# Pooled attention and a gated conv FFN: a ninth conv quarter moves from TensorE to VectorE, under a new order of all engines

## Chip, cores and metric

One Trainium2 chip, one core. The metric is the device time of one execution in microseconds (us); lower is better. Engines are named as in the profile: PE is TensorE's matmuls, PEld its weight loads, DVE is VectorE, ACT is ScalarE, POOL is GpSimd, SP is SyncE.

## What is computed

Eight sequences, each with 8 heads, 576 positions and 64 columns per head. Attention in which keys and values are averaged over groups of 8 positions (so 72 of each per head), and behind it a feed-forward part whose hidden layer is gated by a 3-tap convolution of itself along the sequence:

```python
k_p = k.reshape(B, H, 72, 8, D).mean(axis=3)
v_p = v.reshape(B, H, 72, 8, D).mean(axis=3)
scores = scale * q @ k_p.transpose(0, 1, 3, 2)
attn = softmax(scores)                      # over 72 pooled keys
x = heads_side_by_side(attn @ v_p)          # 8 x 576 x 512
h = relu(x @ w_in)                          # 512 -> 1024
conv = sum(conv_w[t] * shift(h, t - 1) for t in range(3))   # per channel, along the sequence
out = (h * sigmoid(conv)) @ w_out           # 1024 -> 512
```

Inputs and output are f32 in HBM (q, k, v are 9.4 MB each, the output too); the work inside is in bf16 with f32 sums.

## The kernel before, in words

Everything goes by sequence b (0 to 7), and two sequences make a group g that shares a tile gT for the gated hidden layer; channels lie on partitions in blocks fb of 128, positions along the free axis. Four blocks are a **quarter** (b, f4): f4 = 0 holds blocks 0 to 3, f4 = 1 blocks 4 to 7. So 16 quarters of conv in all, two for each sequence.

Attention for a sequence: q, k and v come by loads on POOL's queue (L285, L292, L318, L321; some raw f32 by SP at L300, cast at L307). DVE averages pairs of positions (keys L465; values L512, then L516 masks them). TensorE transposes q (L542, or L546 in smaller pieces) and L560 copies the result from PSUM on DVE or ACT. Scores are matmuls of L608 (16 small ones) or L621 (4 large ones). DVE takes row maxima (L634) and subtracts (L646); ACT takes exponentials (L683). The weights are transposed on TensorE (L693, copied at L707) or by DMA. L718 multiplies by the pooled values, L731 takes the reciprocals of the sums, L746 (DVE) or eight L739 (ACT) divide. L763 transposes x and L771 copies it, again on DVE or ACT; later groups do it by DMA.

FFN for a sequence: `ffn_in` (L776, 64 matmuls 128x288: eight blocks, two half sequences, four pieces of the 512 inputs), `ffn_relu` on ACT (L785) into hT. The convolution of a quarter then has two forms:

- **On TensorE**: `ffn_conv`, two calls per quarter, each 32 matmuls of 64x64 diagonals (L940) over hT. ACT squashes from PSUM (four L965); half the channels land on the other partitions and go to a tile tg first. DVE adds 1 (one L980 for the straight half, two L982 for the crossed one).
- **Taps on DVE**: the ends of each half sequence are first copied beside it (`ffn_wrap`, L860 and L861, two wraps per quarter, on POOL or ACT), then for each block two scalar_tensor_tensor (`ffn_tap`, L912, eight per quarter) sum h·ratio + h into f32 in tg. ACT squashes from tg with the weight as scale (`ffn_tap_tanh`, four L922), and `ffn_tap_gate` (one L927) adds 1.

The tables `Graph.TAPS` (quarters whose taps are on DVE), `Graph.WRAP` (sequences whose hT holds the wrapped ends) and `Graph.SIG` (all quarters of sequences 5 to 7: squashed by a sigmoid itself, so that no 1 is added) say which. Both forms end in `ffn_times` (L990, DVE, gate times h for a quarter). The last matmul L998 takes a group's 128-row tiles, eight matmuls each; L1009 copies the sum from PSUM on DVE or ACT (into osb, or into spare qp buffers), and L1021 stores it. L425 are fillers: matmuls on nothing that keep TensorE going.

Nothing decides at run time. All operations form a graph with dependences, and `Graph.order` emits them in a fixed list, `ORDER`: each number is 2 × operation + choice of engine (where an operation can run on two), −1 a filler. `FORMS` picks forms of scores and transposes, `PLACES` the buffer that each tile gets. An engine's instructions run strictly in the order of that list, so it sets who stands behind whom on each queue. Buffers per ring: tg 3, hT 2, gT 2, v 3, kk 1, qp 4, osb 5.

Of the kernel before, what the change touches and what calls it, by code (L numbers as in the profile page):

```python
# [33 lines left out]
class Graph:  # L34
# [24 lines left out]
    WRAP = (4, 5, 6, 7)  # L59
    TAPS = ((4, 0), (4, 1), (5, 0), (5, 1), (6, 0), (6, 1), (7, 0), (7, 1))  # L60
# [123 lines left out]
def kernel(  # L184
# [1125 lines left out]
    def add_ffn(b, w):  # L1310
# [38 lines left out]
        for f4 in range(n_fb // 4):  # L1349
            if (b, f4) not in Graph.TAPS:  # L1350
                continue
# [148 lines left out]
```

## Time and profile before

| | |
|---|---|
| median of 3 runs | 211.93 us (211.72 to 212.32) |
| the profiled execution, its own time | 211.99 us |
| its span in the trace | 210.3 us |
| granted TensorE clock, mean | 0.996 |
| busy PE / PEld / DVE / ACT / POOL | 199.0 / 135.0 / 191.6 / 170.5 / 43.0 us |
| HBM read / written | 32.52 / 9.44 MB |

The span is what the trace covers, 1.7 us less than the time. Busy time counts instructions of an engine, without the ones that only wait or issue. A matmul is pipelined, so what it counts as busy may include a wait for its place; a step (the time of a run of equal matmuls by their number) is the better measure. In a row "idle before" is the engine's time without work just ahead of the instruction, with what ended it.

### The profile page before, as it was taken

What the parts mean: (1) busy time and instruction counts of PE and PEld (TensorE: products, weight loads), DVE (VectorE), ACT (ScalarE), POOL (GpSimd) and SP (SyncE); (2) the same over time, 40 slices, a digit from 0 to 9 for tenths busy, and PEclk for the clock granted to TensorE, in tenths of its full rate; (3) what the DMA queues carried; (4) which work ended last, traced back from release to release, by engine and by line L of the source; (5) the groups of instructions that cost most, each with busy time, mean ns of one, the idle gap of its engine ahead of it and who ended that gap; (6) DMA issues with size and microseconds to landing.
All of it is one profiled execution on the core that took longest, in us unless ns stands there. A gap on an engine that the chain in (4) does not pass through costs nothing.

```text
span 210.3 us, 6742 instructions
## 1 busy us (share of the span) xinstructions
PE 199.0 (95%) x2764; PEld 135.0 (64%) x2764; DVE 191.6 (91%) x341; ACT 170.5 (81%) x352; POOL 43.0 (20%) x72
## 2 busy tenths in 40 slices
PE   4999999979999999999999999999999999999990
PEld 1567788756688876766768864675577556644450
DVE  7899897999999989999999989999999999999741
ACT  3558886996999889999878999999999998878110
POOL 8823061042311120000000133040026005120000
PEclk9999999999999999999999999999999999999998
DMA  6999999999999999964955865667368547106985
GB/s 205 229 205 208 206 207 208 207 208 205 208 228 206 207 207 202 139 143 84 161 97 104 94 152 115 90 139 149 43 141 183 116 97 180 42 0 141 222 230 158
DMA packets 48835, 33.48 MB, mean 159 GB/s; under 512 B 28300, under 2 KB 43812, under 8 KB 48804
## 3 DMA queue, kind: packets, MB, share of 16 engines
q0 software_dynamic: 15216, 15.40, 44.2%
q1 hardware_dynamic: 32272, 15.67, 36.8%
q10 hardware_dynamic: 1316, 1.98, 3.6%
q8 instruction: 21, 0.34, 0.6%
q14 instruction: 10, 0.08, 0.1%
HBM read 32.52 MB, written 9.44 MB: 200 GB/s over the span
## 4 chain that ended last, share of the span: by engine, by line
PE 63%; DVE 11%; ACT 10%; DMA 8%; issue 4%; ACTq 1%; SPq 0%; DVEq 0%
PE psum L776 21%; PE psum L998 20%; PE psum L718 5%; PE psum L940 5%; DVE negm L634 4%; DVE sd L646 3%; DMA hT<-in_k_dram 3%; DMA out_dram<-qp 3%; PE psum L425 2%; DMA eT<-e 2%; PE psum L608 2%; ACT hT L785 2%; PE psum L693 2%; ACT x L739 2%; PE psum L763 1%
## 5 line engine op out<-in xcount | busy, mean ns | idle before, releaser
L776 PE MATMUL psum<-xT,w_in_sb 128*128 128x288 bf16 x512 | 70.5, 286 | 0.1
L998 PE MATMUL psum<-w_out_sb,gT 128*128 128x512 bf16 (+1 forms) x296 | 67.4, 373 | 0.2 <-DVE gT L990 0.2
L776 PEld LDWEIGHTS <-w_in_sb 128*128 128x128 bf16 x512 | 48.0, 98 | 14.7 <-issue 0.8
L785 ACT ACTIVATE hT<-psum 128x576 bf16<-128x576 f32 x64 | 41.7, 664 | 6.1 <-PE psum L776 5.8
L998 PEld LDWEIGHTS <-gT 128*128 128x128 bf16 x296 | 27.8, 98 | 27.9 <-DVE gT L990 0.7
L860 POOL COPY hT<-hT 128x126 bf16<-128x126 bf16 x13 | 10.2, 786 | 94.2 <-ACT hT L785 90.0
L634 DVE TENSOR_REDUCE negm<-psum 128x8 f32<-128x576 f32 (+2 forms) x37 | 27.4, 746 | 2.1 <-PE psum L608 1.2
L922 ACT ACTIVATE gT<-tg,ratio 128x576 bf16<-128x576 f32 x32 | 25.2, 803 | 2.5 <-DVE tg L912 2.3
L912 DVE SCALAR_TENSOR_TENSOR tg<-hT,ratio 128x576 f32<-128x576 bf16 x32 | 25.5, 813 | 0.7 <-ACT gT L922 0.4
L912 DVE SCALAR_TENSOR_TENSOR tg<-hT,ratio,tg 128x576 f32<-128x576 bf16 x32 | 25.0, 810 | 0.0
L739 ACT ACTIVATE x<-psum,r 128x64 bf16<-128x64 f32 (+1 forms) x96 | 21.2, 357 | 0.4 <-DVE r L731 0.4
L990 DVE TENSOR_TENSOR gT<-gT,hT 128x2304 bf16<-128x2304 bf16 x16 | 21.3, 1346 | 0.1
L646 DVE TENSOR_TENSOR sd<-psum,negm 128x576 f32<-128x576 f32 x27 | 19.9, 747 | 0.6
L718 PE MATMUL psum<-vm,eT 128*128 128x65 bf16 (+5 forms) x240 | 18.7, 222 | 0.4 <-DMA eT<-e 0.4
L683 ACT ACTIVATE e<-sd 128x576 bf16<-128x576 f32 x27 | 18.8, 717 | 0.0
L718 PEld LDWEIGHTS <-eT 128*128 128x128 bf16 (+1 forms) x240 | 15.1, 101 | 4.0 <-DMA eT<-e 0.7
L746 DVE TENSOR_TENSOR x<-psum,r 128x512 bf16<-128x512 f32 (+1 forms) x25 | 16.8, 683 | 0.3
L1009 ACT COPY osb<-psum 128x512 f32<-128x512 f32 x26 | 15.6, 632 | 0.9 <-PE psum L998 0.8
L940 PE MATMUL psum<-hT,dw 64*64 64x288 bf16 (+2 forms) x512 | 15.4, 255 | 0.6 <-ACT hT L785 0.3
L425 PE MATMUL psum<-gT 128*128 128x448 bf16 x40 | 12.8, 419 | 2.8 <-DVE gT L1107 2.8
L940 PEld LDWEIGHTS <-dw 64*64 64x64 bf16 x512 | 12.8, 107 | 2.5 <-issue 2.0
L512 DVE TENSOR_TENSOR v<-v 128x1280 bf16<-128x1280 bf16 (+2 forms) x24 | 12.8, 535 | 0.3
(95 smaller groups left out, 236.5 us busy)
## 6 DMA issues: line engine op xcount, KB each, us to landing
out_dram<-osb SPq DMA_DIRECT2D x54, 128.0 KB, 2.4
v<-in_v_dram POOLq DMA_DIRECT2D x8, 512.0 KB, 16.8
qp<-in_q_dram POOLq DMA_DIRECT2D x7, 576.0 KB, 17.3
kk<-in_k_dram POOLq DMA_DIRECT2D x3, 1152.0 KB, 15.2
out_dram<-qp ACTq DMA_DIRECT2D x14, 128.0 KB, 2.7
hT<-in_k_dram SPq DMA_DIRECT2D x2, 576.0 KB, 5.2
w_in_sb<-in_moe_w_in_dram POOLq DMA_DIRECT2D x2, 512.0 KB, 17.3
w_out_sb<-in_moe_w_out_dram POOLq DMA_DIRECT2D x1, 1024.0 KB, 18.0
```

Of the source, the lines that this page charges most:

```text
L634: nc.vector.tensor_reduce(out=a["m"][0:rows], in_=a["s"][0:rows, :, 0:2 * KW].rearrange("p a (h s) -> p a h s", s=Sp), axis=AX.X, op=OP.ma ...
L646: nc.vector.tensor_tensor(out=a["d"][0:rows], in0=a["s"][0:rows, :, 0:2 * KW].rearrange("p a (h s) -> p a h s", s=Sp), in1=a["m"][0:rows]. ...
L683: nc.scalar.activation(out=dst, in_=src, func=ACT.Exp,)
L718: nc.tensor.matmul(out=a["o"][lo:hi, h // 4, (h % 4) * (D + 1):(h % 4 + x1 - x0) * (D + 1)], lhsT=a["eT"][:, j, lo:hi], rhs=buf("vm", b)[: ...
L739: nc.scalar.activation(out=a["x"][0:rows, n * D:(n + 1) * D], in_=ov[:, n // 4, n % 4, 0:D], func=ACT.Identity, scale=r[0:rows, n // 4, n ...
L776: nc.tensor.matmul(out=banks(ps)[:, j, 0:SC], lhsT=w_in_block(dc, fb), rhs=buf("xT", g)[:, dc, i * S + j * SC:i * S + (j + 1) * SC], start ...
L785: nc.scalar.activation(out=h_of(b)[:, fb].rearrange("p (a s) -> p a s", a=2), in_=banks(ps)[:, :, 0:SC], func=ACT.Relu, scale=1.0 if (b, f ...
L912: nc.vector.scalar_tensor_tensor(out=acc, in0=h, scalar=w, in1=acc if tap else mid, op0=OP.mult, op1=OP.add)
L922: nc.scalar.activation(out=gate, in_=acc_of(b, fb, ps), func=squash(b, fb), scale=ratio[:, 1, fb:fb + 1])
L940: nc.tensor.matmul(out=banks(pss[r ^ c])[c * D:(c + 1) * D, j, lo:hi], lhsT=dw[r * D:(r + 1) * D, tap * n_fb + fb, :], rhs=hT[r * D:(r + 1 ...
L990: nc.vector.tensor_tensor(out=gate, in0=gate, in1=h_of(b)[:, four], op=OP.mult)
L998: nc.tensor.matmul(out=bank(ps)[0:rows, columns], lhsT=buf("gT", g)[:, fb, t * P:t * P + rows], rhs=w_out_sb[:, fb, columns], start=(fb == 0),
```

## The change

It puts quarter (3, 1), the second of sequence 3, into `TAPS`, and sequence 3 into `WRAP`. `ORDER`, `FORMS` and `PLACES` are other tables throughout, found anew; the code that reads them is the same. The diff without the three tables:

```diff
-    WRAP = (4, 5, 6, 7)
-    TAPS = ((4, 0), (4, 1), (5, 0), (5, 1), (6, 0), (6, 1), (7, 0), (7, 1))
+    WRAP = (3, 4, 5, 6, 7)
+    TAPS = ((4, 0), (4, 1), (5, 0), (5, 1), (6, 0), (6, 1), (7, 0), (7, 1), (3, 1))
...
     ORDER = (
-        0, 16, 4, 24, 44, 12, 14, 10, 36, -1, -1, -1, -1, -1, -1, 42, 8, 38, 34, 32,
```

What the two lists hold on each engine, where it differs:

| line | before | after |
|---|---|---|
| L940 PE (conv) | 512 | 448 |
| L542 / L546 PE (q transposed) | 72 / 288 | 126 / 180 |
| L608 / L621 PE (scores) | 376 / 56 | 408 / 44 |
| L425 PE (fillers) | 40 | 40 |
| L912 DVE (taps) | 64 | 72 |
| L927 / L980 / L982 DVE (+1) | 2 / 8 / 16 | 3 / 7 / 14 |
| L922 / L965 ACT (squash) | 32 / 32 | 36 / 28 |
| L860 and L861, POOL | 13 each | 14 each |
| L860 and L861, ACT | 3 each | 4 each |
| L771 DVE / ACT, 512 columns | 5 / 12 | 1 / 16 |
| L560 DVE / ACT, 1152 columns | 4 / 6 | 2 / 8 |
| L560 DVE, 512 columns | 2 | 1 |
| L307 DVE | a q cast, 512 columns | a k cast, 1152 columns |
| L707 DVE, 320 columns | 0 | 1 |
| L1009 DVE / ACT, 512 columns | 7 / 28 | 4 / 31 |

Three places show what moved. The first is DVE where sequence 3's stage begins. The tiles hT_116 and hT_117 are the two buffers of hT, gT_121 and gT_122 of gT; negm and sd are a row maximum and the shifted scores, kk and v the pooled pairs of keys and values. Before, from the second multiply of the sequence ahead of it on:

```order
L990 TENSOR_TENSOR gT_121<-gT_121,hT_116 128x4x576
L634 TENSOR_REDUCE negm_97<-psum 128x8
L465 TENSOR_TENSOR kk_78<-kk_78 128x9x256
L646 TENSOR_TENSOR sd_130<-psum,negm_97 128x576
L465 TENSOR_TENSOR kk_78<-kk_78 128x9x128
L512 TENSOR_TENSOR v_87<-v_87 128x5x128
L634 TENSOR_REDUCE negm_95<-psum 128x8
```

After, from the same multiply on (hT's two buffers have changed places):

```order
L990 TENSOR_TENSOR gT_121<-gT_121,hT_117 128x4x576
L634 TENSOR_REDUCE negm_96<-psum 128x8
L912 SCALAR_TENSOR_TENSOR tg_120<-hT_116,ratio 128x576
L912 SCALAR_TENSOR_TENSOR tg_119<-hT_116,ratio 128x576
L646 TENSOR_TENSOR sd_128<-psum,negm_96 128x576
L912 SCALAR_TENSOR_TENSOR tg_120<-hT_116,ratio,tg_120 128x576
L912 SCALAR_TENSOR_TENSOR tg_119<-hT_116,ratio,tg_119 128x576
L731 RECIPROCAL r_113<-psum 128x8
```

Four of the eight new taps stand between a row maximum and the work of the next tiles; the pooling of kk comes later. The second place is DVE where sequence 3's quarters are gated and multiplied. Before:

```order
L990 TENSOR_TENSOR gT_122<-gT_122,hT_117 128x4x576
L731 RECIPROCAL r_113<-psum 128x8
L512 TENSOR_TENSOR v_88<-v_88 128x5x64
L746 TENSOR_TENSOR x_110<-psum,r_113 128x512
L980 TENSOR_SCALAR gT_122<-gT_122 128x2x576
L982 TENSOR_SCALAR gT_122<-tg_119 64x2x576 x2
L990 TENSOR_TENSOR gT_122<-gT_122,hT_117 128x4x576
```

After:

```order
L980 TENSOR_SCALAR gT_122<-gT_122 128x2x576
L982 TENSOR_SCALAR gT_122<-tg_118 64x2x576 x2
L731 RECIPROCAL r_113<-psum 128x8
L912 SCALAR_TENSOR_TENSOR tg_119<-hT_116,ratio,tg_119 128x576
L990 TENSOR_TENSOR gT_122<-gT_122,hT_116 128x4x576
L516 TENSOR_TENSOR vm_90<-v_88,mask_wide 128x15x64
L927 TENSOR_SCALAR gT_122<-gT_122 128x4x576
L990 TENSOR_TENSOR gT_122<-gT_122,hT_116 128x4x576
```

The second quarter's +1 is now one L927 and its last tap stands ahead of the first quarter's multiply. The third place is the loads on POOL's queue in the head, after the first keys of sequence 1. Before:

```order
L285 DMA qp_74<-in_q_dram 128x4x576
L285 DMA qp_76<-in_q_dram 128x4x576
L328 DMA w_in_sb_67<-in_moe_w_in_dram 128x4x512
L318 DMA v_88<-in_v_dram 128x4x512
L321 DMA v_88<-in_v_dram 64x512
L328 DMA w_in_sb_68<-in_moe_w_in_dram 128x4x512
```

After:

```order
L285 DMA qp_74<-in_q_dram 128x4x576
L328 DMA w_in_sb_68<-in_moe_w_in_dram 128x4x512
L285 DMA qp_75<-in_q_dram 128x4x576
L318 DMA v_87<-in_v_dram 128x4x512
L321 DMA v_87<-in_v_dram 64x512
L328 DMA w_in_sb_67<-in_moe_w_in_dram 128x4x512
```

One half of w_in (w_in_sb_68) now goes ahead of the second query load, and the other (w_in_sb_67) behind the values. Further down the queue the loads of q and v of sequences 4 to 7 are in another order: q5, v4, q7, v5, q6, v6, kk3, v7 before; v4, v5, q6, q7, v6, q5, kk3, v7 after. The new quarter's wraps stand on POOL behind all of them.

More of the change, by code (lines that the diff above doesn't have):

```diff
@@ L72 @@
     ORDER = (
[55 rows of a table removed]
[55 rows of a table added]
     )
     FORMS = (
-        0, 0, 0, 0, 0, 1, 1, 0, 1, 0, 0, 1, 1, 0, 1, 0, 1, 0, 1, 0, 1, 1, 1, 1, 1, 0, 0, 0, 1, 1, 1, 1, 1, 1, 1, 1, 1, 1, 1, 1,
+        1, 1, 1, 0, 0, 1, 1, 0, 0, 0, 1, 1, 0, 1, 1, 0, 0, 0, 1, 1, 1, 0, 1, 1, 1, 0, 0, 1, 0, 1, 0, 1, 1, 1, 1, 1, 1, 1, 0, 0,
     )
     PLACES = (
[18 rows of a table removed]
[18 rows of a table added]
     )
```

145 rows, old and new, of tables (ORDER, PLACES) are left out of this document.

## The prediction

> **What bounds the kernel now.** I read the page's busy line and its chain first, then the engines by stretches, then the waits of the engine that looked tightest. The busy line:
>
> ```profile
> PE 199.0 (95%) x2764; PEld 135.0 (64%) x2764; DVE 191.6 (91%) x341; ACT 170.5 (81%) x352; POOL 43.0 (20%) x72
> PE 63%; DVE 11%; ACT 10%; DMA 8%; issue 4%; ACTq 1%; SPq 0%; DVEq 0%
> ```
>
> TensorE is busy 95% of the span and holds 63% of the chain, VectorE (DVE) 91%. Both are averages over very different stages, so here is the same by five stretches: the head up to the start of the second multiply of sequence 0 (46.5 us), two stretches in the middle, the stretch in which the conv quarters already run on DVE (from 133 us), and the tail behind the last multiply (from 196.2 us). Columns: length, then busy time of PE, weight loads, DVE, ACT, POOL, the clock, DMA.
>
> ```profile
> 0.00:46.50 46.50, 41.75 (x759) 30.47 (x760) 40.46 (x98) 33.88 (x62) 18.69 (x32) 1.00 1.15 209
> 46.50:92.00 45.50, 44.89 (x856) 33.76 (x855) 44.60 (x78) 40.93 (x77) 7.15 (x14) 1.00 1.21 202
> 92.00:133.00 41.00, 40.56 (x653) 28.61 (x651) 38.72 (x71) 36.54 (x83) 4.60 (x8) 1.00 0.63 110
> 133.00:196.20 63.20, 62.93 (x454) 37.57 (x452) 62.58 (x89) 58.56 (x132) 12.55 (x18) 1.00 0.54 113
> 196.20:210.30 14.10, 8.83 (x48) 4.59 (x48) 5.21 (x9) 0.59 (x1) 0.00 (x0) 0.94 0.76 204
> ```
>
> In the middle three (149.7 us) DVE works 44.60 + 38.72 + 62.58 = **145.9 us and idles 3.8**; ACT works 136.0 and idles 13.7. Two engines are full there at once, because TensorE is full too. That needs a look, since a PE that counts as busy may still be waiting inside a matmul. Matmuls of two lines between 150 and 160 us, and their steps in the chain there:
>
> ```profile
> 150.00:160.00 10.00, 7.55 (x61) 6.00 (x62) 1.00 0.63 135
> 150.00:160.00 10.00, 2.45 (x11) 0.78 (x9) 1.00 0.63 135
> ```
>
> ```profile
> 150.56 0.98 PE psum L776 x8
> ...
> 151.89 1.73 PE psum L998 x8
> ```
>
> The windows are L776's, then L998's. A step is 0.98/8 = 0.122 us for L776 and 1.73/8 = 0.216 for L998: 61 × 0.122 + 11 × 0.216 = 9.8 us of work in 10 us for these two lines alone, and the values' matmuls come on top. TensorE has no slack there, at a granted clock of 1.00.
>
> The Trainium skill, "Perfetto Trace Analysis", section "Identifying the Most-Contended Engine", calls matmul busy time a bad metric and points to the share of weight loads instead. By its measure (64%) TensorE would not be the bound and work taken from it would be worth nothing; the count of steps disagrees, and I go by the count.
>
> So TensorE and DVE are near a joint limit, and the change moves work from the one to the other.
>
> DVE's idle time in the middle, by what ended it:
>
> ```profile
> DVE r L731 <- PE psum L718: 0.9, 1, 0.9
> DVE negm L634 <- PE psum L608: 0.6, 2, 0.4
> DVE tg L912 <- ACT gT L922: 0.4, 2, 0.2
> DVE negm L634 <- ACT osb L1009: 0.3, 1, 0.3
> DVE tg L912 <- POOL hT L860: 0.2, 1, 0.2
> ```
>
> Named waits are 2.4 us of the 3.8; the other 1.4 are gaps of a few hundredths between its instructions.
>
> **The change, part by part.** Durations of DVE's instructions (count, then busy us and mean ns):
>
> ```profile
> L912 DVE SCALAR_TENSOR_TENSOR tg<-hT,ratio 128x576 f32<-128x576 bf16 x32 | 25.5, 813 | 0.7 <-ACT gT L922 0.4 <-POOL hT L860 0.2
> L912 DVE SCALAR_TENSOR_TENSOR tg<-hT,ratio,tg 128x576 f32<-128x576 bf16 x32 | 25.0, 810 | 0.0
> L982 DVE TENSOR_SCALAR gT<-tg 64x1152 bf16<-64x1152 bf16 x16 | 7.9, 492 | 0.2
> L980 DVE TENSOR_SCALAR gT<-gT 128x1152 bf16<-128x1152 bf16 x8 | 3.8, 477 | 0.3 <-ACT gT L965 0.3
> L560 DVE COPY qT<-psum 128x1152 bf16<-128x1152 bf16 x4 | 3.0, 753 | 0.0
> L771 DVE COPY xT<-psum 128x512 bf16<-128x512 bf16 x5 | 2.0, 419 | 0.0
> L927 DVE TENSOR_SCALAR gT<-gT 128x2304 bf16<-128x2304 bf16 x2 | 1.5, 754 | 0.0
> L707 DVE COPY eT<-psum 128x640 bf16<-128x640 bf16 x3 | 1.4, 480 | 0.0
> L560 DVE COPY qT<-psum 128x512 bf16<-128x512 bf16 x2 | 0.8, 420 | 0.9 <-PE psum L542 0.9
> L307 DVE CAST qp<-hT 128x512 bf16<-128x512 f32 x1 | 0.6, 643 | 0.0
> ```
>
> *The quarter on DVE.* Added: 4 × 0.813 + 4 × 0.810 for the taps and 0.754 for the +1 of L927 (quarter (3,1) is not in SIG). Removed: one L980 (0.477) and two L982 (0.984). The multiply L990 stays. 7.25 − 1.46 = **+5.8 us**.
>
> *Copies given from DVE to ACT by the new list, ahead of the last multiply:* four L771 (1.68), two large L560 (1.51), one small (0.42): **−3.6**. The other way go one f32 cast of a key pair's 1152 columns for one of 512 query columns, and a half-size L707. The cast stands in no row of DVE: at least 0.753 (as many columns, bf16) and at most 0.643 × 1152/512 = 1.45; I take 1.2, as part of the 0.643 is fixed, so +0.6 net (0.1 to 0.8). The half L707 lies between 0.24 and 0.48; I take 0.3. Together **+0.9**. Single kT copies that change hands come to under 0.2 and are left out.
>
> Sum for DVE before the last multiply: +5.8 − 3.6 + 0.9 = **+3.1 us**. Up to the second multiply of sequence 0 the list holds about the same DVE work as before, so the 3.1 falls on the middle, most of it where sequence 3 is gated. Its cover is the 3.8 us of idle alone. If that went to nothing, the middle would be 145.9 + 3.1 = 149.0, 0.7 shorter than now; if it stayed whole, 3.1 longer.
>
> *TensorE.* It loses the two L940 calls of the quarter, 32 matmuls each.
>
> ```profile
> 91.06 0.74 PE psum L940 x32
> ```
>
> That is 1.5 us; the smaller q-transposes and score matmuls also change form, and my count of all of them stays within a few tenths. So TensorE's middle becomes about 148.2 us, against DVE's 149.0 with no idle at all. **TensorE's saving cannot show unless DVE gets ahead**: DVE takes over the end.
>
> *ACT.* Its rows:
>
> ```profile
> L922 ACT ACTIVATE gT<-tg,ratio 128x576 bf16<-128x576 f32 x32 | 25.2, 803 | 2.5 <-DVE tg L912 2.3
> L965 ACT ACTIVATE tg<-psum 128x576 bf16<-128x576 f32 x16 | 10.4, 656 | 1.6 <-PE psum L940 1.3
> L771 ACT COPY xT<-psum 128x512 bf16<-128x512 bf16 x12 | 6.9, 592 | 2.5 <-PE psum L763 2.5
> L560 ACT COPY qT<-psum 128x1152 bf16<-128x1152 bf16 x6 | 6.7, 1143 | 0.2 <-PE psum L542 0.2
> L860 ACT COPY hT<-hT 128x126 bf16<-128x126 bf16 x3 | 0.9, 306 | 0.1
> ```
>
> Four L922 instead of four L965: +0.6. A wrap, a copy of L860 and one of L861 alike: +0.6. Four L771: +2.4. Two large L560 and a small one: 2.3 + about 0.6 (half of the large one). The cast and L707 that leave, and an output copy and wider divides that come, about cancel. **About +6 us** into 13.7 of idle, nearly half of its cover in the middle. I cost it at nothing because 7.7 us are left; what it costs if that is too little is a rival below.
>
> *POOL.* Each of two quarter halves needs its wrapped ends; one more wrap is POOL's, one ACT's.
>
> ```profile
> L860 POOL COPY hT<-hT x13: 290/790/2262, 119.7 to 187.2; 128x126 bf16<-128x126 bf16 x13
> L912 DVE SCALAR_TENSOR_TENSOR tg<-hT,ratio x32: 759/808/912, 121.0 to 191.4; 128x576 f32<-128x576 bf16 x32
> ```
>
> ```profile
> 76.77 0.56 POOL L321 DMA_DIRECT2D v<-in_v_dram  x1
> ```
>
> ```profile
> 100.55 0.45 DVE L980 TENSOR_SCALAR gT<-gT 128x1152 bf16<-128x1152 bf16 x1
> ```
>
> (First fence: least/median/greatest ns, first and last start; the others: start and length.) The new wrap stands on POOL behind the last load, which before was issued at 77.3 us, and the first tap of (3,1) stands on DVE ahead of sequence 3's first +1, which now starts at 100.6; 27 of DVE's instructions lie between them, at its mean of 191.6/341 = 0.56 us some 15 us, so the tap comes near 85. A late wrap would hold the whole of DVE, score maxima and divides behind it included, as the queue runs in order. A wrap costs 0.8 + 0.8 us on POOL and has some 6 us of cover, so I take nothing, and put the upper end of its cost at the 0.2 us that DVE now loses to L860; if the loads ran 6 us later, DVE would lose what is beyond.
>
> The copy takes 290 ns at best and 790 in the median, while the tap's spread is 759 to 912: it is POOL that pays when the two meet. The Trainium skill, "SBUF — State Buffer", section "Who interferes with whom", says that a DVE instruction with two SBUF inputs and a GpSimd instruction that reads SBUF lock each other out wholly, whoever issues first winning. By that rule two more POOL copies could hold DVE twice for a copy's 0.29, 0.6 us in all; by the row at most twice 0.1, and I keep the row.
>
> *Loads.* The list puts one half of w_in ahead of q2 and swaps later q and v loads. Nothing in the middle waits for a load in the rows above. I cost the later swaps at nothing: each load stays tens of us ahead of its use. The head is not so clear, below.
>
> **Sum.** Middle = 145.9 + 3.1 + idle. Of the 3.8 of idle I keep the 1.4 of gaps, which come with the instructions (as many as before), and a quarter of the 2.4 of waits, since a later DVE finds most of its inputs ready: 2.0. That is 151.0 against 149.7, **+1.3 us**. The profiled execution took 211.99 us, of which 210.3 are span and 1.7 lie outside; the median of the runs shown is 211.93, the same within 0.1. Tail: the same 48 matmuls of L998 behind the last multiply, 8.83 us in the row of the tail. So 211.93 + 1.3 = **213.2 us**, with 212.7 to 215.0 as this case's own range (idle from about 1.5 up to unchanged 3.8).
>
> **The rivals.** What a measurement of this kernel can tell from no change is about 0.3%, 0.64 us.
>
> *ACT becomes the bound too (slower still).* 136.0 + 6 = 142 us; were it to keep 11 of its 13.7 us of idle, because most of that is waiting for TensorE and DVE in turn, the middle is 153, +3.3: 215.2. For: its copies release PSUM banks to TensorE. Against: half its waits go when it is later. Halfway, near 214.5.
>
> *The idle is absorbed (no change).* The stretch from 133 us shows 63.20 − 62.58 = 0.6 us of idle, 1%; DVE can run that tightly. With about 0.9 us over the whole middle it takes 149.9: +0.2, 212.1. For: a list sought anew fits the instructions to each other. Against: the stretch 92 to 133, where the quarter goes, now has 2.3 of 41.
>
> *The head gets shorter (faster).* Ahead of the second multiply of sequence 0 both engines are loose:
>
> ```profile
> 43.44 0.73 PE L425 MATMUL psum<-gT 128*128 128x448 bf16 x3
> 45.21 0.69 PE L542 MATMUL psum<-ident,qp 128*64 128x128 bf16 x18 [1.05 <-issue]
> 46.85 1.35 DVE L990 TENSOR_TENSOR gT<-gT,hT 128x2304 bf16<-128x2304 bf16 x1
> ```
>
> L425 are fillers that compute nothing, and behind them TensorE waits 1.05 us. The head holds 46.50 − 40.46 = 6.0 us of DVE idle. If w_in, sooner, brings that multiply from 46.85 to 44.8, everything behind it moves by 2.0: 1.3 − 2.0 = −0.7, **211.2**. The point from which it decides: a multiply that starts over 1.3 us earlier, near 45.5, gains; over 1.9 earlier it shows. The same follows if the idle shrinks and the head gains 1. For: loads are nearly full in the head (209 GB/s), so their order matters. Against: the work ahead of it is the same.
>
> **How the numbers follow.** Forecast (DVE is late, 212.7 and above) 0.42, ACT too 0.10, absorbed 0.20, head 0.28. The likeliest is 213.2. The range needs 8 in 10: it reaches down to 210.8 (the head by another 0.4) and up to 215.2 (the ACT case's price), which leaves out a few hundredths at each end and what I have not thought of. Slower 0.42 + 0.10 = 0.52, within 0.3% 0.20, faster 0.28.
>
> **What would show it.** Right: DVE's busy time ahead of the last multiply up by about 3 us, TensorE's idle or fillers up by about as much as the time plus 1.5, DVE waits in the middle down toward 2 us, the second multiply of sequence 0 near 46.9 us. Wrong: that multiply well before 45.5; DVE waits above 4 us, on ACT or on POOL's wrap in front of the taps of sequence 3; taps slower than 0.85 us each; a load that ends a wait of TensorE between 60 and 100 us.

## The result and the profile after

The changed kernel takes **210.53 us** (median of 5 runs, 210.06 to 211.23) against 211.87 before (median of 5, 211.70 to 212.32): ratio 0.9942, 95% interval 0.9924 to 0.9959, faster by 0.6%. The prediction was slower, 213.2, in a range from 210.8 up. Direction and range were both missed. One execution of e14 below, at a granted clock of 0.76, took 253.79 us and is left out of its median.

The page of the changed kernel, its busy line and its chain:

```profile
PE 197.2 (95%) x2650; PEld 134.3 (64%) x2666; DVE 190.4 (91%) x338; ACT 174.5 (84%) x363; POOL 45.5 (22%) x74
PE 49%; DVE 24%; ACT 16%; issue 5%; DMA 3%; SPq 0%; DVEq 0%; ACTq 0%
```

Busy shares are close to those of before (PE's 197.2 is a little low: 16 of the kernel's 296 matmuls of L998 are missing from this trace); the chain is not. DVE's share of it went from 11% to 24%, and the DMA's from 8% to 3%. For the place of the gain, cut both executions at the same two events: the start of the second multiply (L990) of sequence 0, and the end of the last multiply. The stretches of before, cut so:

```profile
0.00:46.85 46.85, 42.10 (x761) 30.67 (x762) 40.81 (x98) 34.20 (x63) 18.69 (x32) 1.00 1.15 209
46.85:196.19 149.34, 148.04 (x1957) 99.74 (x1954) 145.53 (x236) 135.70 (x289) 24.31 (x40) 1.00 0.77 139
196.19:210.30 14.11, 8.83 (x48) 4.59 (x48) 5.22 (x10) 0.59 (x1) 0.00 (x0) 0.94 0.76 204
```

And of the changed kernel:

```profile
0.00:45.24 45.24, 41.36 (x795) 30.63 (x795) 39.45 (x98) 32.00 (x53) 16.13 (x29) 1.00 1.15 211
45.24:194.17 148.93, 147.01 (x1825) 99.07 (x1827) 147.49 (x236) 140.78 (x309) 29.32 (x45) 1.00 0.77 141
194.17:208.30 14.13, 8.83 (x48) 4.62 (x48) 3.43 (x6) 1.75 (x3) 0.00 (x0) 0.90 0.69 206
```

Of the 2.0 us between the spans the **head** gives 1.61, the **middle** 0.41, the **tail** nothing. In the middle DVE works 147.49 − 145.53 = 2.0 us more, and its idle time falls from 3.81 to 1.44. The profiled execution of the changed kernel took 210.06 us, the fastest of its five, and the medians differ by 1.34, so about 0.6 of the 2.0 is scatter between executions. The head's part is not: in the eight traces with the changed kernel's head (this one, e1 to e4, e13, e16, e17 below) the multiply starts at 45.18 to 45.57 us, in the four with the old head (before, e5, e11, e12) at 46.85 to 47.09.

Why the head is shorter is seen on two engines. DVE (first fence) and POOL (second) in the changed kernel, ahead of that multiply:

```profile
43.70 0.45 DVE L980 TENSOR_SCALAR gT<-gT 128x1152 bf16<-128x1152 bf16 x1
44.16 0.92 DVE L982 TENSOR_SCALAR gT<-tg 64x1152 bf16<-64x1152 bf16 x2
45.12 0.20 DVE L731 RECIPROCAL r<-psum 64x8 f32<-64x8 f32 x1
45.24 1.30 DVE L990 TENSOR_TENSOR gT<-gT,hT 128x2304 bf16<-128x2304 bf16 x1
```

```profile
45.27 1.03 POOL L292 DMA_DIRECT2D kk<-in_k_dram  x1 [10.60 <-DVE gT L982]
```

And in the kernel before:

```profile
43.91 0.70 DVE L980 TENSOR_SCALAR gT<-gT 128x1152 bf16<-128x1152 bf16 x1
44.62 1.52 DVE L982 TENSOR_SCALAR gT<-tg 64x1152 bf16<-64x1152 bf16 x2
46.18 0.76 DVE L560 COPY qT<-psum 128x1152 bf16<-128x1152 bf16 x1
```

```profile
43.32 1.04 POOL L292 DMA_DIRECT2D kk<-in_k_dram  x1 [10.72 <-PE psum L471]
44.35 0.77 POOL L285 DMA_DIRECT2D qp<-in_q_dram  x1
45.11 0.76 POOL L318 DMA_DIRECT2D v<-in_v_dram  x1
```

Up to 43.7 us the two run level (the L746 ahead of these rows starts at 42.96 us before and at 43.09 after). Then before, L980 and the two L982 take 2.22 us instead of 1.37 while POOL issues three loads beside them, and an L560 copy of 0.7 us stands between them and the multiply. The rest of the 1.61 is small shifts. The new list gives that copy to ACT, and POOL's first issue starts when the +1 is done.

### The profile page after: what moved, and what is told of

It reads as the page before. It is cut to its first block, busy times and chain, and to the rows that moved or that the text cites. A ratio compares the mean times of both kernels' runs of the same rounds, so it can differ in the third digit from the quotient of the medians.

```text
span 208.3 us, 6540 instructions
## 1 busy us (share of the span) xinstructions
PE 197.2 (95%) x2650; PEld 134.3 (64%) x2666; DVE 190.4 (91%) x338; ACT 174.5 (84%) x363; POOL 45.5 (22%) x74
## 4 chain that ended last, share of the span: by engine, by line
PE 49%; DVE 24%; ACT 16%; issue 5%; DMA 3%; SPq 0%; DVEq 0%; ACTq 0%
PE psum L776 19%; PE psum L998 13%; DVE tg L912 6%; DVE negm L634 4%; ACT x L739 4%; PE psum L718 3%; DVE gT L990 3%; DVE sd L646 3%; DMA hT<-in_k_dram 3%; PE psum L940 2%; ACT hT L785 2%; PE psum L693 2%; PE psum L608 2%; ACT gT L922 2%; ACT qT L560 2%
## 5 line engine op out<-in xcount | busy, mean ns | idle before, releaser
L998 PE MATMUL psum<-w_out_sb,gT 128*128 128x512 bf16 (+1 forms) x280 | 65.9, 373 | 1.1 <-issue 0.2
L998 PEld LDWEIGHTS <-gT 128*128 128x128 bf16 x296 | 27.7, 98 | 27.5 <-DVE gT L990 0.6
L860 POOL COPY hT<-hT 128x126 bf16<-128x126 bf16 x14 | 11.3, 810 | 84.2 <-issue 43.6
L912 DVE SCALAR_TENSOR_TENSOR tg<-hT,ratio 128x576 f32<-128x576 bf16 x36 | 28.2, 813 | 0.5 <-ACT gT L922 0.2
L912 DVE SCALAR_TENSOR_TENSOR tg<-hT,ratio,tg 128x576 f32<-128x576 bf16 x36 | 28.2, 810 | 0.0
L922 ACT ACTIVATE gT<-tg,ratio 128x576 bf16<-128x576 f32 x36 | 27.4, 793 | 0.8 <-DVE tg L912 0.7
L990 DVE TENSOR_TENSOR gT<-gT,hT 128x2304 bf16<-128x2304 bf16 x16 | 21.4, 1348 | 0.1
L739 ACT ACTIVATE x<-psum,r 128x64 bf16<-128x64 f32 x96 | 21.2, 356 | 0.1
L1009 ACT COPY osb<-psum 128x512 f32<-128x512 f32 x27 | 16.4, 620 | 4.3 <-PE psum L998 2.7
L683 ACT ACTIVATE e<-sd 128x576 bf16<-128x576 f32 x27 | 19.4, 719 | 0.1
L746 DVE TENSOR_TENSOR x<-psum,r 128x512 bf16<-128x512 f32 (+1 forms) x25 | 16.6, 679 | 0.2
L425 PE MATMUL psum<-gT 128*128 128x448 bf16 x40 | 12.7, 425 | 2.8 <-DVE gT L1107 2.8
L940 PE MATMUL psum<-hT,dw 64*64 64x63 bf16 (+2 forms) x448 | 13.2, 255 | 0.2 <-ACT kT L505 0.2
L940 PEld LDWEIGHTS <-dw 64*64 64x64 bf16 x448 | 10.9, 107 | 2.1 <-issue 1.5
```

Of the source, the lines that this page charges most:

```text
L683: nc.scalar.activation(out=dst, in_=src, func=ACT.Exp,)
L739: nc.scalar.activation(out=a["x"][0:rows, n * D:(n + 1) * D], in_=ov[:, n // 4, n % 4, 0:D], func=ACT.Identity, scale=r[0:rows, n // 4, n ...
L912: nc.vector.scalar_tensor_tensor(out=acc, in0=h, scalar=w, in1=acc if tap else mid, op0=OP.mult, op1=OP.add)
L922: nc.scalar.activation(out=gate, in_=acc_of(b, fb, ps), func=squash(b, fb), scale=ratio[:, 1, fb:fb + 1])
L940: nc.tensor.matmul(out=banks(pss[r ^ c])[c * D:(c + 1) * D, j, lo:hi], lhsT=dw[r * D:(r + 1) * D, tap * n_fb + fb, :], rhs=hT[r * D:(r + 1 ...
L990: nc.vector.tensor_tensor(out=gate, in0=gate, in1=h_of(b)[:, four], op=OP.mult)
```

## The experiments

Each was compared with the kernel before on its own chip (211.72 to 211.84 there, so differences to the 210.53 of another chip hold to about 0.2 us). Start, middle and tail are those of the profiled execution, cut as above; the time is the median.

| run | edit | us | ratio (95%) | start | middle | tail |
|---|---|---|---|---|---|---|
| before | | 211.87 | 1 | 46.85 | 149.34 | 14.11 |
| after | | 210.53 | 0.9942 (0.9924–0.9959) | 45.24 | 148.93 | 14.13 |
| e1 | after, TensorE +1.95 | 212.76 | 1.0046 (1.0029–1.0062) | 45.36 | 150.81 | 15.33 |
| e2 | after, TensorE −1.95 | 210.76 | 0.9955 (0.9938–0.9973) | 45.18 | 149.31 | 14.41 |
| e3 | after, DVE +1.6 | 212.67 | 1.0039 (1.0028–1.0050) | 45.49 | 150.89 | 14.52 |
| e4 | after, DVE −3.2 | 210.95 | 0.9955 (0.9940–0.9970) | 45.57 | 149.02 | 14.41 |
| e5 | before, five copies to ACT | 214.38 | 1.0133 (1.0109–1.0157) | 46.95 | 151.93 | 13.42 |
| e6 | before, head copy to ACT | 212.28 | 1.0026 (1.0015–1.0038) | 46.34 | 150.83 | 13.53 |
| e7 | before, POOL held | 212.20 | 1.0018 (1.0006–1.0031) | 45.95 | 149.39 | 14.86 |
| e8 | e6 and e7 | 212.49 | 1.0035 (1.0022–1.0048) | 45.32 | 151.65 | 13.63 |
| e9 | after, head late | 214.06 | 1.0096 (1.0069–1.0124) | 47.64 | 148.74 | 14.42 |
| e10 | e7 and e11 | 211.03 | 0.9965 (0.9948–0.9981) | 46.43 | 149.63 | 13.44 |
| e11 | before, free buffers | 211.57 | 0.9981 (0.9970–0.9993) | 46.98 | 149.49 | 13.43 |
| e12 | e11, TensorE −1.1 | 210.93 | 0.9963 (0.9949–0.9978) | 47.09 | 148.74 | 13.47 |
| e13 | after, quarter's load back | 213.31 | 1.0059 (1.0037–1.0080) | 45.39 | 150.82 | 15.59 |
| e14 | after, head copy on DVE | 211.10 | 0.9968 (0.9955–0.9980) | 46.15 | 148.81 | 14.44 |
| e15 | e10 and e12 | 210.44 | 0.9934 (0.9913–0.9956) | 46.02 | 148.84 | 13.94 |
| e16 | after, two stores earlier | 209.56 | 0.9890 (0.9873–0.9907) | 45.53 | 148.87 | 13.30 |
| e17 | e16, a tail copy on DVE | 209.64 | 0.9904 (0.9885–0.9924) | 45.22 | 148.91 | 13.38 |

### Which engine sets the middle of the changed kernel

e1, in `ffn_in`:

```diff
-        for dc in range(n_dmc):
+        for n, dc in enumerate((0, 1, 0, 1, 2, 3) if b == 3 and fb >= 4 else range(n_dmc)):
...
-                stop=(dc == n_dmc - 1),
+                stop=(dc == n_dmc - 1 or b == 3 and fb >= 4 and n == 1),
```

> The changed kernel with 16 more matmuls of L776 in sequence 3 (two of the four input pieces summed twice for its blocks 4 to 7; the first sum is thrown away): 16 x 0.122 = 1.95 us more TensorE work in the middle, the other engines' work unchanged. Changed kernel: 210.5. Theory P (TensorE's work sets the middle, the gain came from the 64 matmuls that left it): 212.4. Theory D (VectorE sets it, TensorE's part of the change is hidden): 210.5 to 211.0.

e2, the same place:

```diff
-        for dc in range(n_dmc):
+        for dc in (2, 3) if b == 3 and fb >= 4 else range(n_dmc):
...
-                start=(dc == 0),
+                start=(dc == 0 or b == 3 and fb >= 4 and dc == 2),
```

> The changed kernel with 16 fewer matmuls of L776 in sequence 3 (its blocks 4 to 7 use two of the four input pieces only, so part of x @ w_in is left out): 1.95 us less TensorE work in the middle. Theory P: 208.6 to 209.5 (VectorE's idle of 1.4 us is what can still shrink). Theory D: 210.5, no change.

e3, in `ffn_tap`:

```diff
-        nc.vector.scalar_tensor_tensor(
-            out=acc, in0=h, scalar=w, in1=acc if tap else mid, op0=OP.mult, op1=OP.add
-        )
+        for _ in range(2 if b == 3 and fb < 6 and tap == 0 else 1):
+            nc.vector.scalar_tensor_tensor(
+                out=acc, in0=h, scalar=w, in1=acc if tap else mid, op0=OP.mult, op1=OP.add
+            )
```

> The changed kernel with the first tap of two blocks of quarter (3,1) done twice on VectorE: two L912 more, 2 x 0.813 = 1.6 us. Theory P: 210.5 to 210.9 (taken from VectorE's 1.4 us of idle in the middle). Theory D: 212.1.

e4, ahead of the same call:

```diff
+        if b == 3 and tap == 2:
+            return
         nc.vector.scalar_tensor_tensor(
```

> The changed kernel without the second tap of quarter (3,1) (four L912 left out, so one of the three conv taps is missing there): 4 x 0.810 = 3.2 us less VectorE work in the middle. Theory P: 210.3 to 210.5. Theory D: 207.3 to 209.0, as far as TensorE lets it.

Measured against 210.53: e1 +2.2, e3 +2.1, e2 +0.2, e4 +0.4. The middle of e1, e3, e2 and e4, each from a question of its own:

```profile
45.36:196.17 150.81, 149.86 (x1855) 100.74 (x1843) 147.88 (x236) 141.15 (x309) 30.28 (x45) 1.00 0.77 140
```

```profile
45.49:196.38 150.89, 148.18 (x1840) 99.25 (x1827) 149.14 (x238) 140.80 (x309) 29.27 (x45) 1.00 0.79 140
```

```profile
45.18:194.49 149.31, 147.51 (x1823) 97.98 (x1811) 147.58 (x236) 140.93 (x309) 29.59 (x45) 1.00 0.78 141
```

```profile
45.57:194.59 149.02, 147.92 (x1840) 99.16 (x1827) 144.98 (x232) 140.75 (x309) 29.26 (x45) 1.00 0.77 141
```

Neither theory holds alone. Work **added** to either engine costs all of itself (1.9 us of middle for 1.95, 2.0 for 1.6); work **taken** from one alone brings nothing, and the likely reason is that the other one holds the end. In e2 TensorE's busy time fell by 0.4 only (147.51 against 147.92 in e4, which has all matmuls of the changed kernel) for 1.95 us of matmuls less, so the ones left count more waiting. In e4 DVE has 4.0 us of idle time again and the stretch is no shorter. In this sense the two engines are level; no run relieves both at once. Early in the middle TensorE may have room: 13 of the 40 fillers now stand behind the second multiply, the last at 85.8 us, where before four did, the last at 48.5. Whether they fill gaps or cost time, no run shows.

e13 asks this for the change itself: e1's edit, and additionally

```diff
+        if b == 3 and tap == 2:
+            return
...
-        nc.vector.tensor_scalar(out=gate, in0=gate, scalar1=1.0, scalar2=None, op0=OP.add)
+        if b != 3:
+            nc.vector.tensor_scalar(out=gate, in0=gate, scalar1=1.0, scalar2=None, op0=OP.add)
```

> The changed kernel with about the quarter's load put back: 16 more matmuls of L776 in sequence 3 (1.95 us of TensorE, thrown away, as in e1), and on VectorE without the second tap and the +1 of quarter (3,1) (4 x 0.810 + 0.75 = 4.0 us less; that part of the conv and of the gate is left out). If TensorE's work sets the middle whatever VectorE does: 212.3 to 212.8, as e1, so the quarter's move is worth its TensorE time. If e1's cost came only because VectorE had no slack to follow a later TensorE: 210.8 to 211.5.

It took 213.31. Its middle:

```profile
45.39:196.21 150.82, 148.92 (x1839) 100.75 (x1842) 144.48 (x231) 141.16 (x309) 29.29 (x45) 1.00 0.76 139
```

With DVE's work in the middle down by 3.0 us, the added TensorE time still makes the middle 1.9 us longer, as in e1. There TensorE's time near sequence 3 is worth what it lasts, whatever DVE has left to do. The rest of the 2.8 us lies in the tail, which is 1.5 us longer than the changed kernel's (1.2 in e1's profiled execution, its slowest); why was not tested. The new order without the quarter's move was not run; e13 comes nearest to it.

### The copies that went to ACT

e5 and e6 flip choices of engine in `ORDER` of the kernel before. Three of e5's four L771 stand in this line (998, 976, 812); the fourth (1020) and the L560 (268) are flipped alike:

```diff
-        808, 682, 680, 666, 996, 668, 974, 952, 810, 998, 253, 255, 251, 257, 670, 1170, 976, 955, 166, 812,
+        808, 682, 680, 666, 996, 668, 974, 952, 810, 999, 253, 255, 251, 257, 670, 1170, 977, 955, 166, 813,
```

> The kernel before with five of its copies given from VectorE to ACT, as the changed kernel has them: four L771 of group 1 and the L560 of sequence 5; nothing else moved. VectorE's work in the middle falls by 4 x 0.419 + 0.753 = 2.4 us, ACT's rises by 3.5. Theory B (in the kernel before, too, VectorE and TensorE end together, so relief of one alone gives little): 211.5 to 211.9. Theory D (VectorE alone was the bound before, and these copies are the gain): 209.9 to 210.7. Theory A (ACT's copies come later than VectorE's did): above 212.2.

e6, the L560 ahead of the multiply:

```diff
-        -1, -1, 234, 584, 462, -1, 490, -1, 225, 219, 587, 223, 221, 236, -1, -1, 566, 522, 84, 62,
+        -1, -1, 234, 584, 462, -1, 490, -1, 225, 219, 587, 223, 221, 237, -1, -1, 566, 522, 84, 62,
```

> The kernel before with the one L560 copy that stands ahead of the second multiply of sequence 0 (the q of sequence 3) given to ACT. The multiply should start 0.67 us earlier, at 46.2. Theory H (the gain of the change came from that multiply's earlier start, since everything behind it moves): 211.2 to 211.4. Rival R (both engines have enough else to do then, and the middle sets the end): 211.8 to 212.0.

Both got slower: 2.7 us and 0.6 us against their chip's 211.72. In e6 the multiply did start 0.5 us earlier, but the middle grew by 1.5: behind ACT's other work the copy started at 46.69 us, where DVE had started it at 46.18, and TensorE waited for it (L781 is L763 here, L578 is L560):

```profile
PE psum L781 <- ACT qT L578: 0.7, 1, 0.7
```

In the middle of the kernel before TensorE has no such wait. In e5 it waits 0.7 us for an L560 copy of ACT, too, and 1.0 for a copy of keys. Theory A holds for e5, and e6, above both of its ranges, shows the same: in the old order the handing over of copies is no gain by itself. In the new order one such copy is worth 0.6 us (e14, below); the others were not tested there.

### The head and the tail of the kernel before

e7 makes POOL wait for the product:

```diff
     def load_pair(g):
...
+        if g == 2:
+            nc.gpsimd.tensor_copy(out=buf("kk", g)[:, 0, POOL * D:POOL * D + 8], in_=buf("gT", 0)[:, 3, 0:8])
```

> The kernel before with POOL held, by a copy of 8 columns that reads the product, until the second multiply of sequence 0 is done; so the three loads that POOL issued from 43.3 to 45.9 us (second key pair, then q and v) are issued from about 47.3 on, and none lies beside the +1 of that quarter. If those issues stretched L980 from 0.45 to 0.70 and the two L982 from 0.92 to 1.52 us, the three take 1.37 again and the multiply starts 0.85 earlier, at 46.0. Theory H: 211.0 to 211.2. Rival R: 211.8 to 212.0. Rival S (the stretch has another cause): L982 stays at 0.76 each.

DVE in e7 (its lines stand 20 further down: L1000 is L980, L1002 is L982, L580 is L560, L1010 is L990):

```profile
43.91 0.40 DVE L1000 TENSOR_SCALAR gT<-gT 128x1152 bf16<-128x1152 bf16 x1
44.32 0.92 DVE L1002 TENSOR_SCALAR gT<-tg 64x1152 bf16<-64x1152 bf16 x2
45.27 0.76 DVE L580 COPY qT<-psum 128x1152 bf16<-128x1152 bf16 x1
45.95 1.35 DVE L1010 TENSOR_TENSOR gT<-gT,hT 128x2304 bf16<-128x2304 bf16 x1
```

The +1 takes 0.40 and 0.92 us, 0.90 less than before: **POOL's load issues had stretched it**. The multiply starts 0.90 earlier and the last one 0.85, the middle being the same (149.39). Yet the time did not fall; the tail grew to 14.86 us. The end of e7's chain of waits (start, length, what):

```profile
200.75 0.77 ACTq L1041
201.52 0.04 issue
201.56 3.31 DMA out_dram<-qp
204.86 0.03 issue
204.89 0.05 DVEq L1029
204.94 0.04 issue
204.99 0.42 DVE qp L1029
```

The last copy (L1029 is L1009) waited until 204.86 us for a store that still read the buffer it writes, when the last matmul had ended at 195.40 + 8.83 = 204.23:

```profile
195.40 8.83 PE L1018 MATMUL psum<-w_out_sb,gT 128*128 128x512 bf16 x48 [0.19 <-DVE gT L1010]
```

The kernel before has the same chain, a hair ahead of its matmuls:

```profile
202.15 2.71 DMA out_dram<-qp
204.85 0.03 issue
204.88 0.05 DVEq L1009
204.93 0.04 issue
204.98 0.42 DVE qp L1009
```

The changed kernel has no store in it; its taps, last multiply, matmuls and copy follow each other:

```profile
184.34 7.29 DVE tg L912 x10
191.63 2.55 DVE gT L990 x2
194.18 0.05 issue
194.23 8.84 PE psum L998 x48
203.07 0.02 issue
203.09 0.42 DVE qp L1009
```

e8 joins e6 and e7:

> Both at once in the kernel before: the L560 of sequence 3 on ACT and POOL held until the multiply is done. The multiply should start 1.5 us earlier, at 45.3, as in the changed kernel (45.24), without the quarter moved. Theory H: 210.3 to 210.6, all of the gain. Rival R: 211.6 to 212.0, and the gain needs the quarter's 1.5 us off TensorE.

At 212.49 it lies above both ranges: the multiply starts at 45.32, as predicted, and all of it is lost to e6's longer middle. Read alone, e6 to e8 would have said that the head is worth nothing. e10 and e11 free the tail first, by four numbers of `PLACES`, the buffers of the last four tiles; e10 has e7's edit too:

```diff
-        1, 3, 5, 0, 0, 2, 2, 6, 3, 0, 5, 6,
+        1, 3, 5, 2, 0, 2, 2, 6, 4, 7, 1, 6,
```

> The kernel before with those four buffers alone, POOL as it was. In its tail the matmuls end at 205.08 and the last copies wait for stores until 204.98, so either alone gives the end. Theory T: 211.5 to 211.9, at most 0.2 less. If the buffers alone were the gain of the change: 210.5.

> The kernel before with POOL held until the second multiply of sequence 0 (as in e7) and with the last four output tiles copied into buffers that no store still reads (four numbers of PLACES). Theory T (in e7 the 0.85 us were lost in the tail, where copies waited for stores out of the same buffers): 210.9 to 211.2. Rival (e7's loss lay elsewhere): 211.7 to 212.2.

211.57 and 211.03: the buffers alone bring 0.2 (the tail of that execution 0.7), and on top of them the same POOL edit that was worth nothing in e7 brings 0.5. Theory T stands. (In e10's trace the L560 copy waits 0.55 us for TensorE, so the multiply starts at 46.43 and not at 46.0.)

e12 adds to e11, in `ffn_conv`:

```diff
-                    if n >= len(todo[j]):
+                    if n >= len(todo[j]) or n and b == 3 and f2 >= 2:
...
-                            stop=(n == len(todo[j]) - 1),
+                            stop=(n == len(todo[j]) - 1 or b == 3 and f2 >= 2),
```

> The kernel before with those four buffers, and with quarter (3,1)'s convolution on TensorE cut to its middle tap (two of three taps left out): 48 of its 64 matmuls less, 48 x 0.023 = 1.1 us of TensorE; VectorE and ACT as before. Theory P (before the change TensorE set the middle and VectorE had its 3.8 us of idle): 210.6 to 210.9. Theory B (both end together before, too): 211.5 to 211.9.

210.93, 0.6 less than e11 for 1.1 us of TensorE: theory P for the most part. Before the change TensorE was the tighter of the two engines, and DVE's idle time was room. e15 is all three parts:

> The kernel before with three parts together: the four free buffers in the tail, POOL held until the second multiply of sequence 0, and quarter (3,1)'s conv cut to its middle tap (two taps left out: 1.1 us less TensorE). Alone, the buffers gave about 0.2, POOL 0.5 more, TensorE 0.6 more. If they add: 210.3 to 210.6, the time of the changed kernel. If they are bought out of the same slack: 210.9 to 211.1.

210.44, the time of the changed kernel: buffers, head and TensorE's relief add up. It is not the same sum: the changed kernel has more from the head (1.61 us against 0.83) and nothing from the tail.

### The head of the changed kernel

e9 does the two L982 of the second-multiplied quarter of sequence 0 three times, in `ffn_gate`:

```diff
-        for r in range(2):
+        for r in (0, 1) * (3 if (b, f4) == (0, 0) else 1):
```

> The changed kernel with the two L982 of the second-multiplied quarter of sequence 0 done three times over: four more, 4 x 0.455 = 1.8 us of VectorE just ahead of that multiply, which should start at 47.1 instead of 45.24 us. Theory H (what is late at that multiply stays late to the end): 212.0 to 212.4. Rival R (the engines have other work then, and the middle takes it up): 210.5 to 211.0.

e14 flips one choice in `ORDER`:

```diff
-        462, -1, -1, 237, 582, 216, 262, 221, 584, 464, 82, 225, -1, -1, 219, -1, 223, -1, -1, 265,
+        462, -1, -1, 236, 582, 216, 262, 221, 584, 464, 82, 225, -1, -1, 219, -1, 223, -1, -1, 265,
```

> The changed kernel with the L560 copy of sequence 3's q that the new list gave to ACT back on VectorE, ahead of the second multiply of sequence 0: that starts 0.7 us later, at 45.9 to 46.0. Theory H (a late head stays late): 211.1 to 211.4. Rival (ACT, free of 1.15 us, makes up for it): 210.3 to 210.8.

e14: multiply 0.91 later (0.25 of it stands ahead of the copy already), time 0.6 more. e9: multiply 2.40 later, last multiply 2.21 later, so nearly all of the lateness is carried through the middle. Its median rose by 3.5 us, far above theory H's range; the profiled execution is its fastest (212.47 of 212.47 to 214.61, at a mean granted clock of 0.995), and why the others (0.988 to 0.994) were slower stays open. That the multiply came 2.4 instead of 1.8 later has a reason of its own. DVE, then POOL, in e9:

```profile
44.14 3.34 DVE L982 TENSOR_SCALAR gT<-tg 64x1152 bf16<-64x1152 bf16 x6
```

```profile
45.22 1.03 POOL L292 DMA_DIRECT2D kk<-in_k_dram  x1 [10.61 <-DVE gT L982]
```

Six L982 at 0.455 would be 2.7 us; they took 3.34, with one load issue of POOL beside them. That is the stretch again, put there by accident.

### A version faster than both

The changed kernel's tail is 0.7 us longer than e11's. Its DMA, between two stretches of matmuls (columns as above):

```profile
192.00:194.00 2.00, 2.00 (x10) 0.78 (x8) 2.00 (x2) 1.40 (x3) 0.00 (x0) 1.00 0.01 1
194.00:196.00 2.00, 1.90 (x10) 0.83 (x10) 0.77 (x2) 0.59 (x1) 0.00 (x0) 1.00 0.04 11
```

Next to nothing is stored for 4 us, while two finished tiles of the last group wait behind later tiles in the queues of SP and ACT. e16 moves their two stores right behind their copies, both on SP (1944 moves up behind 1943, 1921 behind 1919 and becomes 1920); e17 also flips 1707 to 1706, a copy that ACT makes late behind its own store issues.

```diff
-        1731, 2036, 1723, 1732, 1914, 2022, 2038, 1916, 2016, 2024, 2052, 1694, 2018, 1943, 1932, 1919, 2026, 1696, 1934, 2078,
-        1699, 1937, 1700, 2054, 2056, 1707, 1944, 1921, 2080, 1708, 2070, 2082, 2058, 2062, 2085, 1724, 2072, 2061, 2064, 2074,
+        1731, 2036, 1723, 1732, 1914, 2022, 2038, 1916, 2016, 2024, 2052, 1694, 2018, 1943, 1944, 1932, 1919, 1920, 2026, 1696,
+        1934, 2078, 1699, 1937, 1700, 2054, 2056, 1707, 2080, 1708, 2070, 2082, 2058, 2062, 2085, 1724, 2072, 2061, 2064, 2074,
```

> The changed kernel with the stores of two output tiles of the last group (copied at 192.4 to 193.4 us) issued by SP right behind their copies, where now they stand behind stores of later tiles and leave from 196 us on; nothing else moved. Theory S (the tail of the changed kernel is bound by stores that pile up behind 196 us): the tail falls from 14.1 to 13.4 us, the time to 209.8 to 210.1. Rival M (the 48 matmuls and the last copy bound it): 210.4 to 210.7.

> The same with one more edit: the copy of a tile of group 2 that ACT makes at 196.28 us, 1.5 us late behind its own store issues, goes to VectorE, which has nothing to do then. Theory S: 0 to 0.3 us less than e16. Rival: no difference from e16.

SP's stores in e16, and its windows:

```profile
193.17 2.40 SPq L1021 DMA_DIRECT2D out_dram<-qp  x4
```

```profile
192.00:194.00 2.00, 2.00 (x11) 0.88 (x9) 2.00 (x2) 1.63 (x3) 0.00 (x0) 1.00 0.09 21
194.00:196.00 2.00, 1.90 (x10) 0.72 (x9) 1.00 (x2) 0.58 (x1) 0.00 (x0) 1.00 0.75 175
```

The tail falls to 13.30 us and the time to **209.56**, 1.1% under the kernel before (0.9873 to 0.9907). Theory S holds, by more than it said; e17 adds nothing.

## Why the prediction was wrong, step by step

The forecast of +1.3 us was a middle of +1.3, and a head and a tail of nothing. Measured were −0.41, −1.61 and 0.02. Two terms failed by about as much, 1.6 us in the head and 1.7 in the middle, and either would have turned the sign: with the head right the sum is −0.3, with the middle right −0.4.

- **"Up to the second multiply of sequence 0 the list holds about the same DVE work as before"**: this step failed for the head. DVE's busy time there fell from 40.81 to 39.45 us. There are 98 instructions on DVE in both heads, but not the same ones (a 0.75 us L560 fewer just ahead of that multiply), and not at the same durations: the mean of L982 hid two instructions of 0.76 us among fourteen of 0.455. The multiply starts 1.61 us earlier, of which 0.85 is the stretch that is gone and 0.7 the copy. e14 and e9 show in the changed kernel that this start is carried to the end, e10 in the kernel before.
- **The head as a rival** had the right sign and point of decision (a multiply before 45.5 us gains) at a chance of 0.28, and the wrong mechanism. Its 211.2 came near by luck: with the 1.61 us its sum gives 1.3 − 1.61 = −0.3, and the middle did the rest. No part of w_in is seen: the first multiply starts 0.49 us earlier (40.62 against 41.11), but by the L746 at 43 us that is gone again.
- **"TensorE's saving cannot show unless DVE gets ahead"**: wrong as the only bound. e12 shows 0.6 us of gain for 1.1 of TensorE before the change, e1 and e13 a middle longer by 1.9 us if TensorE's time comes back. The count of steps (9.8 us of work in 10 us) had said that TensorE was full; the forecast then let DVE's sum override it.
- **DVE +3.1 us in the middle**: this term, too, failed. The durations of the instructions that start there do sum to 3.5 us more: five L771 left the middle, not four, but only one large L560, not two; the other one, the small one, the cast (0.92 us, forecast 1.2) and the L707 belong to the head. Yet DVE's busy time there rose by 2.0 only. A duration counts some 0.06 to 0.07 us in which an instruction overlaps the next one; instructions that used to have a gap behind them now overlap, so adding durations overstates what they occupy. Over head and middle together DVE's busy time rose by 0.6 us (186.34 to 186.94), where the prediction's sign was about 3.
- **Idle kept, 2.0 us**: 1.44, so the other part of the middle's miss. The 1.4 of gaps were not fixed to the instructions. With 2.0 + 1.4 in place of 3.1 + 2.0 the forecast's own sum gives 145.5 + 2.0 + 1.4 − 149.3 = −0.4, the measured middle. (A slip on which nothing rests: halfway between 213.2 and 215.2 is 214.2, not 214.5.)
- **ACT at nothing** held in the new order: 5.1 us more of work in the middle (140.78 − 135.70). In the old order five of the same copies cost 2.7 (e5). That the list and the copies belong together was not in the forecast.
- **Tail "the same"**: the same length, for another reason. Before, stores and matmuls ended together; after, stores pile up behind an idle stretch.
- POOL's one more wrap was hidden, as said: DVE waits 0.2 us on L860 in both kernels. TensorE waits for no load, and the taps keep 0.81 us.

The contention was in the trace of the kernel before. The Trainium skill, "SBUF — State Buffer", section "Who interferes with whom", says that copies and tensor_scalar in their two-port modes and GpSimd lock each other out for a whole instruction, and that the order of issue decides who waits. The traces agree that such instructions pay: L980 0.70 and L982 0.76 us beside POOL's load issues, 0.40 and 0.46 without them (e7). They do not show a wait for a whole issue, as the stretch is 0.30 us beside issues of 0.76 to 1.04. L990, a tensor_tensor, kept 1.30 us beside an L292. The forecast used that section for the taps, where the price was small, and not for the instructions it names.

## What to carry to other kernels

Add a little work to each engine, then take a little away: if adding costs on two engines and taking away helps on neither, they are level. Then look for a change that starts or ends the whole stretch sooner, as gained here, or that relieves both, which was not tried. Ahead of a level stretch, look up each instruction's own duration on the last few microseconds instead of its mean, and see what POOL issues beside it. When an edit moves an event earlier and the time doesn't follow, look at the tail's store queue before calling the edit worthless.

## What the runs showed of the hardware

- A load issue on POOL stretches DVE's bf16 tensor_scalar that runs beside it: 128x1152 from 0.40 (e7) or 0.45 (changed kernel) to 0.70 us, 64x1152 from 0.46 to 0.76 us; holding POOL back took the stretch away (e7), and adding such instructions beside an issue brought it back (e9: 0.6 us for one issue of 1.03 us). A copy out of PSUM beside an issue kept its time (L560, 0.76 us in e14 and in e7).
- Stores are issued in the order of their queue: two finished tiles left at 195.98 and 196.31 us, behind tiles that were not finished; when they went first they left at 193.17 and 194.4, and the time fell by 1.0 us (e16 against the changed kernel).
- A busy TensorE is no good measure of its load: 16 matmuls or 1.95 us fewer lowered its busy time in the middle by 0.4 us (147.51 in e2, 147.92 in e4).
